# Preset ones for the warming products, and another split of the weights' narrowing, in a fused attention and gated feed-forward kernel

## The chip, the cores and the metric

The kernel runs on one core of one Trainium2 chip. A core has five engines with queues of their own: TensorE (PE) for matrix products, VectorE (DVE), ScalarE (ACT), GpSimd (POOL) and SyncE (SP), the last here used to issue transfers. The metric is the device time of one execution in microseconds. Times below that have a line number are those of the kernel before the change.

## The reference

Attention by a polynomial sketch, then a gated feed-forward layer:

```python
def phi(x):                       # x: batch 4, heads 4, sequence 1088, head dimension 32
    a = einsum('rd,bhsd->bhsr', S1, x)      # r = 8
    b = einsum('rd,bhsd->bhsr', S2, x)
    return outer product of a and b, 64 features
q_p, k_p = phi(q), phi(k)
kv  = einsum('bhsf,bhsd->bhfd', k_p, v)
z   = sum of k_p over s
num = einsum('bhsf,bhfd->bhsd', q_p, kv)
den = einsum('bhsf,bhf->bhs', q_p, z) + 1e-06
x   = (num / den), heads joined: 4352 tokens x 128
out = (sigmoid(x @ w_gate) * (x @ w_val)) @ w_out     # 128 -> 1536 -> 128
```

q, k and v are 32-bit. S1, S2, w_gate, w_val and w_out come as 64-bit floats; the kernel reads them as pairs of 32-bit integers and makes 32-bit floats of them itself.

## The kernel before

**Feed-forward.** The 4352 tokens are cut into chunks of 512 and the 1536 inner columns into 12 blocks of 128. A wave (`w1`, products at L364) makes gate and val of one block for one chunk: two products of 128x512 into one PSUM tile `wave`. ACT takes the sigmoid of gate (`sg`, L372), DVE multiplies with val (`g`, L388). `w2` (L321, tile `moeout`) multiplies the block's g with its w_out and adds over the 12 blocks. `slot` orders them: at each turn the product g of the last wave, then the `moeout` of two waves back, then the next wave. After the twelfth, DVE turns the sum (`o_sb`, L331) and SP writes it out. Products of 32-bit floats appear in the profile as two records each.

**Attention** fills x, transposed (`xT`), batch by batch, between the waves. Batch 0 has nothing to hide behind and goes first: k and q are turned on DVE (`kT` L432, `qT` L443), S is turned on PE (`st`, L812), and from it come `sk` (L823), `kps`, `gram`, `kp`, `dps` (the denominators), `kvz` (k_p times v, L647), `kvd` (a copy on ACT, L683), `ndps` (L717), `nd` (a copy on ACT, L730), `nps` (the numerators, L758) and `xT` (L785). The denominators pass through `dT` (DVE, L750) and `rc` (ACT, L873). The products of ones (`warm`, L262) into a scratch tile give nothing to the result; there are three at the start, one behind `st`, one ahead of `dps`, and one ahead of the first wave.

**Narrowing** (`narrow`) makes 32-bit floats out of pairs in four steps, each placed by hand in the order of the program: step 0 is `cap` on POOL (L97) and `tail` on ACT (L101), the two that read the raw pairs `w_in`; step 1 is two DVE operations on `head` (L105, L109); step 2 is `square` on ACT (L117) and the addition on POOL (L118); step 3 is the DVE write of `w_sb` (L127). Before the change `narrow_01` takes blocks 0 and 1 in three parts (gate and val of 0; gate and val of 1; out of 0 and 1), and `narrow_w(j)` takes gate, val and out of one block j. The engines are scheduled by hand: each executes its instructions in the order in which the program wrote them.

**Loads.** SP issues all loads of weights in one order: gate and val of block 0, v of batch 0, gate and val of block 1, out of 0 and 1, the rest of q, and then gate, val and out by pairs of blocks. The raw pairs of two blocks lie in one tile `w_in` each, and there are six such tiles (`raw`, `bufs=NJ // 2`). Eight semaphores count the landings in turn; the framework puts in the waits for them, by the slices that an instruction reads and that a load writes. The core functions:

Of the kernel before, what the change touches and what calls it, by code (L numbers as in the profile page):

```python
# [9 lines left out]
I32 = mybir.dt.int32  # L10
# [10 lines left out]
def kernel(  # L21
# [30 lines left out]
    const = ctx.enter_context(tc.tile_pool(name="const", bufs=1))  # L52
    ld = ctx.enter_context(tc.tile_pool(name="ld", bufs=1))
    sbA = ctx.enter_context(tc.tile_pool(name="sbA", bufs=2))
    raw = ctx.enter_context(tc.tile_pool(name="raw", bufs=NJ // 2))
    sbN = ctx.enter_context(tc.tile_pool(name="sbN", bufs=1))
    sbG = ctx.enter_context(tc.tile_pool(name="sbG", bufs=6))

# [83 lines left out]
                nc.sync.dma_start(out=rows, in_=s_)  # L142


    w_sb = const.tile([P, 3, NJ, P], F32, tag="w_sb", name="w_sb")
    w_in = {}

    def load_w_in(j0, j1):
        cs = slice(j0 * P, j1 * P)
        n, jj = divmod(j0, 2)  # L150
        if wide and jj == 0:
            w_in[n] = raw.tile([P, 3, 2, P, 2], I32, tag="w_in", name="w_in")
        for i, src in enumerate((moe_w_gate, moe_w_val)):
            if wide:
                nc.sync.dma_start(
                    out=w_in[n][:, i, jj : jj + j1 - j0].rearrange("p j m w -> p (j m w)"),
                    in_=src[:, cs].bitcast(I32),
                )
            else:
                nc.sync.dma_start(  # L160
                    out=w_sb[:, i, j0:j1].rearrange("p j m -> p (j m)"), in_=src[:, cs]
                )

    def load_w_out(n):
        j0, j1 = 2 * n, 2 * n + 2
        cs = slice(j0 * P, j1 * P)
        src = moe_w_out[cs, :].bitcast(I32) if wide else moe_w_out[cs, :]
        nc.sync.dma_start(
            out=w_in[n][:, 2].rearrange("p j m w -> p j (m w)") if wide else w_sb[:, 2, j0:j1],
            in_=src.rearrange("(j p) m -> p j m", p=P),  # L170
        )

    narrowing = {}

    def narrow_w(j, step):
        if not 0 <= j < NJ:
            return
        n, jj = divmod(j, 2)
        if wide:
            if step == 0:  # L180
                narrowing[j] = narrow(
                    w_sb[:, :, j, :], w_in[n][:, :, jj], nc.gpsimd, "acc1" if j < NJ - 2 else None
                )
            next(narrowing[j])


    def narrow_01(part, step):
        if wide:
            if step == 0:
                i = (slice(0, 2), part) if part < 2 else (2, slice(0, 2))  # L190
                narrowing["01", part] = narrow(
                    w_sb[:, i[0], i[1]],
                    w_in[0][:, i[0], i[1]],
                    nc.gpsimd,
                    "acc0" if part else "acc1",
                )
            next(narrowing["01", part])


    def load_rows(src, b, t, parts=((0, T, nc.sync),)):  # L200
# [48 lines left out]
        load_w_in(2 * n, 2 * n + 2)  # L249
        load_w_out(n)  # L250

    ones = const.tile([P, 32], F32, tag="ones")
    nc.vector.memset(ones, 1.0)


    def warm(*cols):
        t = psm.tile([P, 2, 512], F32, tag="wave", name="warm")
        one = [bass.AP(tensor=ones.tensor, offset=ones.offset, ap=[list(ones.ap[0]), [0, n]]) for n in cols]
        x = bass.AP(tensor=ones.tensor, offset=ones.offset, ap=[list(ones.ap[0]), [0, P]])
        for r in one:  # L260
            n = r.shape[-1]
            nc.tensor.matmul(out=t[:, 0, :n], lhsT=x, rhs=r, start=True, stop=True)  # L262

    sig0 = const.tile([P, 1], F32, tag="sig0")
    nc.scalar.activation(out=sig0, in_=ones[:, :1], func=ACTF.Sigmoid)
    warm(512, 512, 128)
    hm = const.tile([P, 2, R], F32, tag="hm")
    nc.vector.memset(hm, 0.0)  # L268
    for h in range(H):
# [44 lines left out]
    def w2(ci, j0, jn, g):  # L314
        t0, tw = tok_chk[ci]
        if j0 == 0:
            moe["sum"] = ci
            moe["acc"] = pso.tile([P, TCH], F32, tag=f"acc{ci % 2}", name="moeout")
        for jj in range(jn):
            j = j0 + jj  # L320
            nc.tensor.matmul(  # L321
                out=moe["acc"][:, :tw],
                lhsT=w_sb[:, 2, j, :],
                rhs=g[:, jj, :tw],
                start=(j == 0),
                stop=(j == NJ - 1),
            )
        if j0 + jn == NJ:
            o_sb = sbA.tile([P, TCH // 32, 32], F32, tag="o_sb", name="o_sb")
            nt = tw // 32  # L330
            nc.vector.transpose(  # L331
                out=o_sb[:, :nt, :].rearrange("p t d -> p (t d)"), in_=moe["acc"][:, :tw]
            )
            c = t0
            while c < t0 + tw:
                b, r = divmod(c, S)
                n = min(t0 + tw - c, S - r) // 32
                u = (c - t0) // 32
                for g4 in range(4):

                    eng = nc.scalar if ci == len(tok_chk) - 1 and g4 % 2 else nc.sync
                    eng.dma_start(
                        out=bass.AP(
                            tensor=out.tensor,
                            offset=out.offset + (b * S + r // 32) * DM + 32 * g4,
                            ap=[[T * DM, 32], [DM, n], [1, 32]],
                        ),
                        in_=o_sb[32 * g4 : 32 * g4 + 32, u : u + n, :],
                    )
                c += n * 32  # L350

    def w1():

        ci = moe["ci"]
        t0, tw = tok_chk[ci]
        jn = TCH // tw
        j0 = moe["w"] * jn
        wv = psm.tile([P, 2, TCH], F32, tag="wave", name="wave")

        tp = tw // 2 if ci == 0 and j0 == 0 else tw  # L360
        for o in range(0, tw, tp):
            for which in range(2):
                for jj in range(jn):
                    nc.tensor.matmul(  # L364
                        out=wv[:, which, jj * tw + o : jj * tw + o + tp],
                        lhsT=w_sb[:, which, j0 + jj, :],
                        rhs=xT[:, t0 + o : t0 + o + tp],
                        start=True,
                        stop=True,
                    )  # L370
        sg = sbG.tile([P, TCH], F32, tag="sg", name="sg", bufs=3)
        nc.scalar.activation(out=sg, in_=wv[:, 0], func=ACTF.Sigmoid)  # L372
        if ci == 0:
            if j0 == 1:
                narrow_01(2, 3)
            if 0 < j0 < NJ - 2:
                narrow_w(j0 + 1, 3)
            narrow_w(j0 + 2, 1)
            narrow_w(j0 + 2, 2)
            if j0 < 3:  # L380
                narrow_w(j0 + 3, 0)
            if j0 > 1:
                narrow_w(j0 + 4, 0)


        def glu():
            g = sbG.tile([P, TCH], F32, tag="g", name="g")
            nc.vector.tensor_tensor(out=g, in0=wv[:, 1], in1=sg, op=MUL)  # L388
            moe["todo"].append((ci, j0, jn, g.rearrange("p (j t) -> p j t", j=jn)))

        moe["gate"] = glu
        moe["w"] += 1
        if j0 + jn == NJ:
            moe["ci"] += 1
            moe["w"] = 0
# [260 lines left out]
    def kv(b, zsum):  # L656
        kvz = KVZ[b] = ps2.tile([P, 2, 512], F32, tag="two", name="kvz")[:, 0]
        for j in [1, 2, 3, 4, 5, 6, 7, 8, 0]:
            kr = 64 if j == 0 else P
            for h in range(H):  # L660
                nc.tensor.matmul(  # L661
                    out=kvz[32 * h : 32 * h + 32, :F],
                    lhsT=v_t[b][:kr, h, j, :],
                    rhs=KP[b][:kr, h // 2, j, h % 2, :],
                    start=(j == 1),
                    stop=(j == 0),
                    skip_group_check=True,
                )
        for h in range(H):
            nc.tensor.matmul(  # L670
                out=kvz[32 * h : 32 * h + 32, F : 2 * F],
                lhsT=ones,
                rhs=zsum[:, h, :],
                start=False,
                stop=True,
                skip_group_check=True,
            )
# [139 lines left out]
        start=True,  # L817
        stop=True,
    )
    warm(128)  # L820
    st_ = st_[:, : 2 * R].rearrange("p (n r) -> p n r", n=2)
    sk = const.tile([P, 2, 2, R], F32, tag="sk")
    nc.vector.tensor_tensor(  # L823
# [28 lines left out]
    mult10 = ab(None, (0, 1, 0), (psm, "wave"))  # L852
    for pi in range(2):
        outer(0, pi, NJK - 1, NJK, eng=nc.gpsimd)
    for part in range(2):
        narrow_01(part, 0)
    spread_z()
    warm(512)
    for pi in range(2):
# [6 lines left out]
    def rest(turn, rc, dT):  # L866
# [5 lines left out]
        nt = rc.shape[1] - 1  # L872
        nc.scalar.activation(out=rc[:, :nt], in_=dT[:, :nt, :2], func=ACTF.Identity, bias=eps)  # L873
        kvd(0)
        narrow_01(0, 1)
        narrow_01(0, 2)
        ndt(0)

    divide = dn(0, 0, rest)
    warm(256)  # L880

    def head1():
        narrow_01(1, 1)
        narrow_01(0, 3)
        narrow_01(1, 2)
        narrow_01(2, 0)
        narrow_w(2, 0)

    divide((0, 4), (4, 8), between=head1)
    narrow_01(1, 3)  # L890
    narrow_01(2, 1)
    narrow_01(2, 2)

    slot(None, 1)
    cq = {}
# [82 lines left out]
```

## Time and profile before

| | |
|---|---|
| median of 12 runs | 305.53 us (305.18 to 309.55) |
| the profiled execution | 305.94 us |
| its span, first to last instruction | 304.2 us |
| mean granted clock of PE | 0.998 |
| transfers | 23.31 MB, mean 77 GB/s over the span |

The span is what the profile divides; some 1.7 us of the execution lie around it. The busiest groups outside PE, as the page has them (line, engine, operation, output and inputs with shapes, count, then busy us, mean ns, and idle us before them with what ended most of it):

```profile
L388 DVE TENSOR_TENSOR g<-wave,sg 128x512 f32<-128x512 f32 x102 | 70.3, 689 | 128.2 <-ACT sg L372 127.9
L118 POOL TENSOR_TENSOR head<-head,tail 128x384 int32<-128x384 int32 (+2 forms) x14 | 13.4, 955 | 17.8 <-DVE head L109 14.7
L262 PE MATMUL warm<-ones 128*128 128x512 f32 (+2 forms) x12 | 6.8, 698 | 1.0 <-DVE hm L268 1.0
L127 DVE SCALAR_TENSOR_TENSOR w_sb<-square,head 128x384 f32<-128x384 f32 (+1 forms) x11 | 5.7, 518 | 3.9 <-POOL head L118 3.9
L101 ACT ACTIVATE tail<-w_in 128x384 int32<-128x384 uint32 (+1 forms) x13 | 6.6, 521 | 0.5 <-DMA w_in<-in_moe_w_gate_dram 0.5
```

Most of the narrowing runs between 9 and 46 us, in the first chunk's waves. Idle time of DVE, ACT and POOL costs nothing by itself; PE is busy 98% of the span.

### The profile page before, as it was taken

The numbers are of one execution on the slowest core, as the hardware profiler recorded it, in microseconds if no ns is written. First come the engines' busy times: TensorE is split into PE (matmuls) and PEld (weight loads), VectorE is DVE, ScalarE is ACT, GpSimd is POOL, SyncE is SP. The second block draws the span as 40 slices with busy tenths as digits, with TensorE's granted clock in tenths as the row PEclk, the third lists the DMA queues.
The fourth block names the chain that finished last, engine by engine and source line by source line (L and its number), as shares of the span: only waits on it lengthen the run. The fifth ranks groups of instructions, "written<-read, shape, count | busy, mean of one in ns | idle before, by whom it ended". The sixth has DMA issues, their size and how long they took to land.

```text
span 304.2 us, 3619 instructions
## 1 busy us (share of the span) xinstructions
PE 297.3 (98%) x1366; PEld 137.0 (45%) x1366; DVE 154.8 (51%) x267; ACT 81.1 (27%) x150; POOL 35.4 (12%) x65
## 2 busy tenths in 40 slices
PE   8899999999999999999999999999999999999995
PEld 3444434443344444434444445434444444444683
DVE  6997798753756444464365443635232223222331
ACT  3556532222222222211222222221222222222220
POOL 1466540600000500000003100000000000000000
PEclk9999999999999999999999999999999999999999
DMA  7992440998402591450004950200010000100021
GB/s 221 356 336 66 126 144 6 163 152 149 147 4 44 127 181 30 79 174 10 0 12 97 187 89 2 36 0 2 0 21 13 0 0 9 28 0 0 7 31 17
DMA packets 29874, 23.31 MB, mean 77 GB/s; under 512 B 20960, under 2 KB 25056, under 8 KB 29856
## 3 DMA queue, kind: packets, MB, share of 16 engines
q1 hardware_dynamic: 25488, 15.21, 18.6%
q0 software_dynamic: 3456, 7.09, 13.7%
q10 hardware_dynamic: 912, 0.77, 0.9%
q8 instruction: 11, 0.18, 0.3%
q14 instruction: 7, 0.06, 0.1%
HBM read 19.80 MB, written 3.26 MB: 76 GB/s over the span
## 4 chain that ended last, share of the span: by engine, by line
PE 74%; DMA 5%; DVE 1%; issue 0%; DVEq 0%
PE wave L364 46%; PE moeout L321 24%; DMA bq<-dq 5%; PE nps L758 1%; PE dps L739 1%; PE kvz L661 1%; DVE qp L639 0%; PE kps L460 0%; PE cqps L606 0%; DVE g L388 0%; PE kvz L670 0%; DVE o_sb L331 0%; PE ndps L717 0%; DVEq L639 0%
## 5 line engine op out<-in xcount | busy, mean ns | idle before, releaser
L364 PE MATMUL wave<-xT,w_sb 128*128 128x512 f32 (+1 forms) x436 | 191.7, 565 | 0.1
L388 DVE TENSOR_TENSOR g<-wave,sg 128x512 f32<-128x512 f32 x102 | 70.3, 689 | 128.2 <-ACT sg L372 127.9
L364 PEld LDWEIGHTS wave<-xT,w_sb 128*128 128x128 f32 x436 | 82.6, 190 | 93.6 <-issue 86.0
L372 ACT ACTIVATE sg<-wave 128x512 f32<-128x512 f32 x102 | 60.9, 597 | 199.5 <-PE wave L364 199.5
L321 PE MATMUL moeout<-g,w_sb 128*128 128x512 f32 (+1 forms) x216 | 105.5, 576 | 0.6 <-DVE w_sb L127 0.3
L321 PEld LDWEIGHTS moeout<-g,w_sb 128*128 128x128 f32 x216 | 39.4, 190 | 44.5 <-issue 37.2
L630 POOL DMA_DIRECT2D qp<-dq x12 | 7.1, 590 | 110.6 <-DMA dq<-cq 68.6
L118 POOL TENSOR_TENSOR head<-head,tail 128x384 int32<-128x384 int32 (+2 forms) x14 | 13.4, 955 | 17.8 <-DVE head L109 14.7
L639 DVE TENSOR_TENSOR qp<-qp,bq 128x1152 f32<-128x1152 f32 (+1 forms) x7 | 9.1, 1295 | 3.9 <-DMA bq<-dq 3.9
L539 DVE TENSOR_TENSOR kp<-kab 128x1152 f32<-128x1152 f32 (+2 forms) x10 | 10.5, 1069 | 0.0
L262 PE MATMUL warm<-ones 128*128 128x512 f32 (+2 forms) x12 | 6.8, 698 | 1.0 <-DVE hm L268 1.0
L109 DVE SCALAR_TENSOR_TENSOR head<-cap,head 128x384 int32<-128x384 int32 (+2 forms) x14 | 7.5, 534 | 0.5
L127 DVE SCALAR_TENSOR_TENSOR w_sb<-square,head 128x384 f32<-128x384 f32 (+1 forms) x11 | 5.7, 518 | 3.9 <-POOL head L118 3.9
L331 DVE STREAM_TRANSPOSE o_sb<-moeout 128x512 f32<-128x512 f32 (+1 forms) x9 | 6.1, 680 | 2.6 <-PE moeout L321 2.5
L630 POOL DMA_DIRECT2D bq<-dq x12 | 6.9, 579 | 0.3
L101 ACT ACTIVATE tail<-w_in 128x384 int32<-128x384 uint32 (+1 forms) x13 | 6.6, 521 | 0.5 <-DMA w_in<-in_moe_w_gate_dram 0.5
L97 POOL TENSOR_SCALAR cap<-w_in 128x384 f32<-128x384 f32 (+1 forms) x13 | 6.5, 509 | 0.0
L785 DVE TENSOR_TENSOR xT<-nps,rb 128x576 f32<-128x576 f32 (+2 forms) x9 | 5.9, 661 | 0.7
L774 DVE STREAM_TRANSPOSE rb<-rc 128x576 f32<-128x576 f32 (+2 forms) x9 | 6.1, 681 | 0.3
L758 PE MATMUL nps<-qp,nd 64*32 64x256 f32 (+1 forms) x128 | 5.5, 401 | 0.4 <-ACT nd L730 0.4
L443 DVE STREAM_TRANSPOSE qT<-kq 128x512 f32<-128x512 f32 (+1 forms) x8 | 5.7, 714 | 0.0
L739 PE MATMUL dps<-qp,zb 128*32 128x256 f32 (+1 forms) x64 | 5.3, 404 | 0.3 <-DVE zb L529 0.2
(74 smaller groups left out, 84.6 us busy)
## 6 DMA issues: line engine op xcount, KB each, us to landing
qp<-dq POOLq DMA_DIRECT2D x12, 288.0 KB, 9.8
bq<-dq POOLq DMA_DIRECT2D x12, 288.0 KB, 9.8
v<-in_v_dram SPq DMA_DIRECT2D x16, 144.0 KB, 6.6
kq<-in_k_dram SPq DMA_DIRECT2D x3, 544.0 KB, 4.2
kq<-in_q_dram SPq DMA_DIRECT2D x3, 544.0 KB, 5.1
w_in<-in_moe_w_out_dram SPq DMA_DIRECT2D x6, 256.0 KB, 7.0
w_in<-in_moe_w_gate_dram SPq DMA_DIRECT2D x5, 256.0 KB, 5.7
w_in<-in_moe_w_val_dram SPq DMA_DIRECT2D x5, 256.0 KB, 4.9
```

What stands on the lines that cost most here:

```text
L109: nc.vector.scalar_tensor_tensor(out=head, in0=cap, scalar=-0x40000000, in1=head, op0=ALU.bitwise_and, op1=ALU.bitwise_or)
L118: nc.gpsimd.tensor_tensor(out=head, in0=head, in1=tail, op=ALU.add)
L262: nc.tensor.matmul(out=t[:, 0, :n], lhsT=x, rhs=r, start=True, stop=True)
L321: nc.tensor.matmul(out=moe["acc"][:, :tw], lhsT=w_sb[:, 2, j, :], rhs=g[:, jj, :tw], start=(j == 0), stop=(j == NJ - 1),)
L364: nc.tensor.matmul(out=wv[:, which, jj * tw + o : jj * tw + o + tp], lhsT=w_sb[:, which, j0 + jj, :], rhs=xT[:, t0 + o : t0 + o + tp], sta ...
L372: nc.scalar.activation(out=sg, in_=wv[:, 0], func=ACTF.Sigmoid)
L388: nc.vector.tensor_tensor(out=g, in0=wv[:, 1], in1=sg, op=MUL)
L539: eng.tensor_tensor(out=KP[b][:, pi, j0:j1].rearrange("p j m (i l) -> p (j m) i l", i=R), in0=bass.AP(tensor=a0.tensor, offset=a0.offset, ...
L630: get.dma_start(out=t[64 * c : 64 * c + 64, n * H * W1 : (n + 1) * H * W1], in_=bass.AP(tensor=d0.tensor, offset=d0.offset, ap=rows + [[1, ...
L639: nc.vector.tensor_tensor(out=q0, in0=q0, in1=half(BQ[b], n), op=MUL)
L739: nc.tensor.matmul(out=dps[32 * h : 32 * h + 32, :w], lhsT=zb[b % 2][:, h, :], rhs=half(QP[b], n)[:, 2 * (h % 2) + h // 2, :], start=True, ...
L758: nc.tensor.matmul(out=t[32 * h : 32 * h + 32, c, :w], lhsT=ND[b][rows, 32 * h : 32 * h + 32], rhs=half(QP[b], n)[rows, 2 * (h % 2) + h // ...
```

## The change

Three things are changed.

The products of ones, the first sigmoid and the sum of z (L670) no longer read a tile `ones` that DVE fills; they read the constant 1.0 that the framework has POOL write before the kernel's first instruction (at L962 in the profile), with a step of zero. The third leading product and the one behind `st` have 256 columns where they had 128.

The raw weights are one tile instead of six, and both it and `w_sb` are laid out as a row of 38 blocks: gate 0 to 11, val 12 to 23, two places unused, out from 26 on.

The narrowing is split otherwise. gate and val of blocks 0, 1 and 2 go by themselves, out of block 0 goes by itself, and from block 3 on one narrowing takes gate j, val j and out of j - 2, which are places j, j + 12 and j + 24, one slice with a step of 12. A last one takes out of 10 and 11.

```diff
-    raw = ctx.enter_context(tc.tile_pool(name="raw", bufs=NJ // 2))
+    raw = ctx.enter_context(tc.tile_pool(name="raw", bufs=1))
...
-    w_sb = const.tile([P, 3, NJ, P], F32, tag="w_sb", name="w_sb")
-    w_in = {}
+    w_sb = const.tile([P, 3 * NJ + 2, P], F32, tag="w_sb", name="w_sb")
+    w_in = raw.tile([P, 3 * NJ + 2, P, 2], I32, tag="w_in", name="w_in") if wide else None
...
-                    out=w_in[n][:, i, jj : jj + j1 - j0].rearrange("p j m w -> p (j m w)"),
+                    out=w_in[:, i * NJ + j0 : i * NJ + j1].rearrange("p j m w -> p (j m w)"),
...
+        to = slice(2 * NJ + 2 + j0, 2 * NJ + 2 + j1)
...
-            out=w_in[n][:, 2].rearrange("p j m w -> p j (m w)") if wide else w_sb[:, 2, j0:j1],
+            out=w_in[:, to].rearrange("p j m w -> p j (m w)") if wide else w_sb[:, to],
...
-    def narrow_01(part, step):
...
+    def narrow_w(part, step):
+        if wide and part in places:
             if step == 0:
...
+                at, bank = places[part]
+                narrowing[part] = narrow(w_sb[:, at], w_in[:, at], nc.gpsimd, bank)
+            next(narrowing[part])
+
+    places = {j: (slice(j, j + 2 * NJ + 1, NJ), "acc1") for j in range(3, NJ - 2)}
+    places.update({j: (slice(j, j + 2 * NJ + 1, NJ), None) for j in range(NJ - 2, NJ)})
+    places.update({("gv", j): (slice(j, j + NJ + 1, NJ), f"acc{1 - j % 2}") for j in range(3)})
+    places["out", 0] = slice(2 * NJ + 2, 2 * NJ + 3), "acc0"
+    places[NJ] = slice(3 * NJ, 3 * NJ + 2), None
...
-    ones = const.tile([P, 32], F32, tag="ones")
-    nc.vector.memset(ones, 1.0)
...
-        x = bass.AP(tensor=ones.tensor, offset=ones.offset, ap=[list(ones.ap[0]), [0, P]])
+        x = nc.const_aps.tensor(1.0, [P, P], F32)
+        for n in cols:
+            r = nc.const_aps.tensor(1.0, [P, n], F32)
...
-    warm(512, 512, 128)
+    warm(512, 512, 256)
...
-                lhsT=w_sb[:, 2, j, :],
+                lhsT=w_sb[:, 2 * NJ + 2 + j, :],
...
         if ci == 0:
-            if j0 == 1:
-                narrow_01(2, 3)
-            if 0 < j0 < NJ - 2:
-                narrow_w(j0 + 1, 3)
-            narrow_w(j0 + 2, 1)
-            narrow_w(j0 + 2, 2)
+            if j0 == 0:
+                narrow_w(("gv", 2), 1)
+                narrow_w(("gv", 2), 2)
+                narrow_w(("out", 0), 3)
+            else:
+                if j0 == 1:
+                    narrow_w(("gv", 2), 3)
+                elif j0 != NJ - 2:
+                    narrow_w(j0 + 1, 3)
+                narrow_w(j0 + 2, 1)
+                narrow_w(j0 + 2, 2)
...
-    warm(128)
+    warm(256)
...
-    for part in range(2):
-        narrow_01(part, 0)
+    narrow_w(("gv", 0), 0)
+    narrow_w(("gv", 1), 0)
...
-        narrow_01(2, 0)
-        narrow_w(2, 0)
+        narrow_w(("out", 0), 0)
+        narrow_w(("gv", 2), 0)
```

In the built program the order of SP's loads is as before, and no load waits for more than it did. The first `tail` on ACT and the first `cap` on POOL (gate and val of block 0) wait for six load semaphores; before, they waited for three.

More of the change, by code (lines that the diff above doesn't have):

```diff
@@ L142, in load_s @@
                 nc.sync.dma_start(out=rows, in_=s_)
-    w_sb = const.tile([P, 3, NJ, P], F32, tag="w_sb", name="w_sb")
-    w_in = {}
+    w_sb = const.tile([P, 3 * NJ + 2, P], F32, tag="w_sb", name="w_sb")
+    w_in = raw.tile([P, 3 * NJ + 2, P, 2], I32, tag="w_in", name="w_in") if wide else None
     def load_w_in(j0, j1):
         cs = slice(j0 * P, j1 * P)
-        n, jj = divmod(j0, 2)
-        if wide and jj == 0:
-            w_in[n] = raw.tile([P, 3, 2, P, 2], I32, tag="w_in", name="w_in")
         for i, src in enumerate((moe_w_gate, moe_w_val)):
@@ L160, in load_w_in @@
                 nc.sync.dma_start(
-                    out=w_sb[:, i, j0:j1].rearrange("p j m -> p (j m)"), in_=src[:, cs]
+                    out=w_sb[:, i * NJ + j0 : i * NJ + j1].rearrange("p j m -> p (j m)"),
+                    in_=src[:, cs],
                 )
@@ L173 @@
     narrowing = {}
[L175 to L179, printed above, removed]
-            if step == 0:
[L181 to L184, printed above, removed]
-    def narrow_01(part, step):
[L188 to L197, printed above, removed]
+    def narrow_w(part, step):
+        if wide and part in places:
+            if step == 0:
+                at, bank = places[part]
[6 more added lines that the diff above has]
+    places[NJ] = slice(3 * NJ, 3 * NJ + 2), None
     def load_rows(src, b, t, parts=((0, T, nc.sync),)):
@@ L250 @@
         load_w_out(n)
-    ones = const.tile([P, 32], F32, tag="ones")
-    nc.vector.memset(ones, 1.0)
     def warm(*cols):
         t = psm.tile([P, 2, 512], F32, tag="wave", name="warm")
-        one = [bass.AP(tensor=ones.tensor, offset=ones.offset, ap=[list(ones.ap[0]), [0, n]]) for n in cols]
-        x = bass.AP(tensor=ones.tensor, offset=ones.offset, ap=[list(ones.ap[0]), [0, P]])
-        for r in one:
-            n = r.shape[-1]
+        x = nc.const_aps.tensor(1.0, [P, P], F32)
+        for n in cols:
+            r = nc.const_aps.tensor(1.0, [P, n], F32)
             nc.tensor.matmul(out=t[:, 0, :n], lhsT=x, rhs=r, start=True, stop=True)
     sig0 = const.tile([P, 1], F32, tag="sig0")
-    nc.scalar.activation(out=sig0, in_=ones[:, :1], func=ACTF.Sigmoid)
-    warm(512, 512, 128)
+    nc.scalar.activation(out=sig0, in_=nc.const_aps.tensor(1.0, [P, 1], F32), func=ACTF.Sigmoid)
+    warm(512, 512, 256)
     hm = const.tile([P, 2, R], F32, tag="hm")
@@ L365, in w1 @@
                         out=wv[:, which, jj * tw + o : jj * tw + o + tp],
-                        lhsT=w_sb[:, which, j0 + jj, :],
+                        lhsT=w_sb[:, which * NJ + j0 + jj, :],
                         rhs=xT[:, t0 + o : t0 + o + tp],
@@ L671, in kv @@
                 out=kvz[32 * h : 32 * h + 32, F : 2 * F],
-                lhsT=ones,
+                lhsT=nc.const_aps.tensor(1.0, [P, 32], F32),
                 rhs=zsum[:, h, :],
@@ L874, in rest @@
         kvd(0)
-        narrow_01(0, 1)
-        narrow_01(0, 2)
+        narrow_w(("gv", 0), 1)
+        narrow_w(("gv", 0), 2)
         ndt(0)
@@ L882, in head1 @@
     def head1():
-        narrow_01(1, 1)
-        narrow_01(0, 3)
-        narrow_01(1, 2)
-        narrow_01(2, 0)
-        narrow_w(2, 0)
+        narrow_w(("gv", 1), 1)
+        narrow_w(("gv", 0), 3)
+        narrow_w(("gv", 1), 2)
+        narrow_w(("out", 0), 0)
+        narrow_w(("gv", 2), 0)
     divide((0, 4), (4, 8), between=head1)
-    narrow_01(1, 3)
-    narrow_01(2, 1)
-    narrow_01(2, 2)
+    narrow_w(("gv", 1), 3)
+    narrow_w(("out", 0), 1)
+    narrow_w(("out", 0), 2)
     slot(None, 1)
```

## The prediction

> **What bounds the kernel now.** I read the page's busy shares first, then the costliest groups, then the order of time around the start, and last the waits of SP's queue, because the change touches only the first 45 us.
>
> ```profile
> span 304.2 us, 3619 instructions
> PE 297.3 (98%) x1366; PEld 137.0 (45%) x1366; DVE 154.8 (51%) x267; ACT 81.1 (27%) x150; POOL 35.4 (12%) x65
> PE   8899999999999999999999999999999999999995
> L364 PE MATMUL wave<-xT,w_sb 128*128 128x512 f32 (+1 forms) x436 | 191.7, 565 | 0.1
> L321 PE MATMUL moeout<-g,w_sb 128*128 128x512 f32 (+1 forms) x216 | 105.5, 576 | 0.6 <-DVE w_sb L127 0.3
> ```
>
> TensorE is the bound: the idle time ahead of its two large groups sums to 0.7 us (0.1 and 0.6) in the whole span. Whatever moves that first product moves the end by as much. It stands here, in the order of time (the columns are start, duration, engine, line, operation):
>
> ```profile
> 9.24 0.81 ACT L101 ACTIVATE tail<-w_in 128x256 int32<-128x256 uint32 x2 [0.46 <-DMA w_in<-in_moe_w_gate_dram]
> ...
> 12.28 0.31 ACT L873 ACTIVATE rc<-dT,eps 128x16 f32<-128x16 f32 x1 [2.23 <-DVE dT L750]
> 12.93 0.27 ACT L683 COPY kvd<-kvz 128x128 f32<-128x128 f32 x1 [0.34 <-PE kvz L647]
> ...
> 13.93 0.67 PE L758 MATMUL nps<-qp,nd 64*32 64x256 f32 x16 [0.35 <-ACT nd L730]
> 14.53 0.70 PE L262 MATMUL warm<-ones 128*128 128x256 f32 x2
> ```
>
> The first wave product starts at 15.18. Ahead of it on ACT stands the narrowing of blocks 0 and 1 (tail, 9.24), and behind that, in the same queue, the reciprocal's input rc, the copy kvd and the copy nd. Note what ended the 0.46 us before the tail: a gate load. The first tail reads gate and val of block 0 alone, issued at 1.93 and 2.41; but the gate load of block 1 was issued at 4.97, and in the built program this tail waits for it too. Its slice (gate 0 and val 0, two blocks apart) has gate 1 lying between them, and the wait covers what lies between.
>
> The other rows I need are SP's. It issues the last loads of gate at 16.01, and is then held (waits of SP's queue, 20 to 28 us: waiter, what it waited for, us in total, times, longest):
>
> ```profile
> 16.01 0.33 SPq L155 DMA_DIRECT2D w_in<-in_moe_w_gate_dram  x1
> ...
> 20.23 0.31 SPq L215 DMA_DIRECT2D v<-in_v_dram  x1
> SPq L630 <- DMA dq<-cq: 5.0, 1, 5.0
> SPq L630 <- DMA w_in<-in_moe_w_gate_dram: 1.6, 1, 1.6
> ```
>
> So the gate load of blocks 10 and 11 landed at 20.54 + 1.6 = 22.2 us. (Then 5.0 more to 27.2, where the next issue stands at 27.27: the sum closes.)
>
> [...] rc, kvd, nd stand in program order. [...] weight loads for the 512-column ones follow each other by 0.86 us (1.97, 2.83, 3.68), while in the steady part they follow by 0.43 (26.16, 26.59, 27.02). [...]
>
> **The change part by part.**
>
> 1. *w_in becomes one tile of 38 blocks: gate 0-11, val 12-23, two unused, then out.* This is the part that decides. The first narrowing now takes blocks 0 and 12. Between them lie all twelve gate blocks. The changed program's ACT and POOL queues show it: the first tail and the first cap wait for six load semaphores where three stood before, each counted up to the last gate load that uses it, the latest being gate 10-11. Those loads are issued by SP in the old order with no new wait, and SP depends on nothing that ACT now holds (its next wait on compute is the end of kvz on PE, at 12.9, which ACT does not feed). So they land when they did: 22.2. The first tail moves from 9.24 to 22.2. Behind it wait, on ACT: the second tail, rc, kvd, squares, nd; on POOL: both caps; DVE waits at the head of block 0 after dT (11.75), PE at ndps. Two tails take 0.81: rc at 23.0. From rc (12.28) to the first wave (15.18) took 2.90 before; the weights' own path, cap 0.4, DVE 0.25 + 0.42, POOL 0.73, DVE 0.42, is 2.2 plus handovers and runs beside it. First wave at 25.9: **+10.7**. Nothing gives it back, since PE is full afterwards. If the landing moves by 0.7 either way, so does this.
>
> 2. *PE's clock.* PE has nothing between kvz's end (12.87) and ndps (23.6), 10.7 us. I take the half rate from there. ndps 0.33 and nps 0.67 contain some 0.5 of streaming: +0.5. After that the waves run at half rate until about 4.2 us after nps began (the length of the first slow ones, 0.96 to 5.17), that is from 26.4 to 28.6-29: 2.4 us of time does 1.2 us of work: +1.2. The slow PE hides the 0.3 that moeout waited for w_sb: -0.3. **+1.4**; bounds 0.5 (nps counts early and clock is back at 27) and 2.6 (half rate for 4.2 us after 26.4, and nothing hidden).
>
> 3. *out is narrowed two blocks later, with gate and val of j go out of j-2.* moeout of j-2 stands one product (0.86 us) ahead of wave j on PE, so it needs the same w_sb write 0.86 earlier. Before, w_sb for blocks 5 to 9 ended at 28.32, 30.95, 33.57, 36.19, 38.82, and moeout of 3 to 7 started at 27.88, 30.45, 33.02, 35.60, 38.17: each would now be late by 0.4 to 0.65. These are not added: the loop DVE w_sb, 105, 109, POOL head, w_sb turns in 2.62 us by itself against PE's 2.57, so lateness is carried, up to 0.65. Block 11 is worse: w_sb ended at 46.02, moeout of 9 started at 44.94 before; late by 1.08, of which 0.65 has been paid, and the 0.27 that wave 11 waited anyway goes: 0.2 more. Block 12 (out 10 and 11) adds on DVE 0.28 + 0.42 + 0.42, on POOL 0.5 + 0.73, and ends near moeout of 10: 0.1. Together near 0.9; the slow PE at the start lets the loop gain a little on it: **+0.7**; bounds 0 (loop far ahead) and 1.7 (each block pays anew).
>
> 4. *Ones from the constant.* One memset (0.09) and PE's wait for it go: first product 0.1 earlier. The third leading product has 256 columns for 128: at half rate +0.4, so st, at 5.20, comes up to 0.3 later; the one behind st adds up to 0.2 ahead of kps. All this ends by 13.5 and is covered by the wait to 22.2: **0**; without cover up to 0.5.
>
> 5. *Narrower first pieces.* out of block 0 alone (128 columns for 256) and gate and val of 2 (256 for 384) save about 0.5 on DVE and 0.6 on POOL between 16 and 20 of the old time. PE gained at most the 0.3 already taken in step 2: **0**.
>
> Sum: 10.7 + 1.4 + 0.7 = 12.8. The profiled execution took 305.94, of which 1.7 lies around its span of 304.2; it would give 318.7. The median, 305.53, is 0.4 lower: 305.5 + 12.8 = **318.3**.
>
> **The rivals.**
> *The wait bites alone* (chance 0.13): PE gets its clock back at once and w_sb stays ahead: 10.7 or a bit less, 316.0. For: ones and nps precede the first wave; against: 10.7 us of idle.
> *Everything dear* (0.11): clock slow for longer, or loads landing near 23, and each late w_sb paid: 10.7 + 2.6 + 1.7 = 15, 320.5 to 321. For: the loop of 2.62 has no slack[...].
> *The other side* (0.05): the long slice's wait ends before it matters, as it would if the last gate load landed by about 9.8 us, ahead of rc; then the head is unmoved, moeout's 0.3 goes, part 3 returns as much, and the time is 305.2: no change. Against: that load is not even issued until 16.01.
> My forecast, all three terms near their middles, has 0.71.
>
> **How the numbers follow.** The likeliest gives 318.3. The range takes the first rival's middle and half of the dear case: 315.9 to 320.6. What a measurement here can tell from no change is about 0.5%, 1.5 us. Slower holds all but the other side: 0.95; of the rest, same 0.03, faster 0.02.
>
> **What would show it.** In the changed kernel's profile: the first tail near 22.2, waiting some 13 us on a gate load; first wave near 26; PE's third slice of 40 (16 to 24 us) empty; weight loads for the first wave products longer than 0.19; moeout waiting for w_sb in sum 0.5 to 1; everything after 60 us shifted by a constant. Wrong if the tail starts near 9 (then no part of this holds), or if the shift keeps changing after 60 us.

## The result, and the profile after

The changed kernel takes 318.09 us (median of 11 runs, 316.66 to 319.43) against 305.49 (median of 47). The ratio is 1.0405, with a 95% interval of 1.0384 to 1.0426: slower, by 12.6 us. 318.3 was predicted, with 315.9 to 320.6 as the range.

The page of the changed kernel: its span, the busy shares, PE's busy tenths and granted clock in 40 slices of 7.9 us, and the group of the copy `kvd`'s reader.

```profile
span 316.3 us, 3624 instructions
PE 299.5 (95%) x1366; PEld 137.9 (44%) x1366; DVE 155.9 (49%) x269; ACT 80.8 (26%) x152; POOL 35.8 (11%) x67
...
PE   8509999899999999999999999999999999999995
PEclk9956999999999999999999999999999999999999
...
L709 PE MATMUL ndps<-ident,kvd 128*128 128x128 f32 x7 | 1.6, 302 | 10.4 <-ACT kvd L675 10.4
```

PE's busy time has hardly grown (297.3 to 299.5); the span has grown by 12.1. The third slice, 16 to 24 us, is empty, and nearly all new idle time stands before one product, `ndps`, which waits for an ACT copy. The clock row shows a second thing: the granted clock of slices 3 and 4 (15.8 to 31.6 us) is 5 and 6 tenths.

The order of time around the start (start, duration, engine, line, operation, and in brackets the idle time before it and what ended that):

```profile
11.63 0.44 DVE L742 STREAM_TRANSPOSE dT<-dps 128x256 f32<-128x256 f32 x1
...
22.01 0.75 ACT L101 ACTIVATE tail<-w_in 128x256 int32<-128x256 uint32 x2 [13.35 <-DMA w_in<-in_moe_w_out_dram]
22.11 0.78 POOL L97 TENSOR_SCALAR cap<-w_in 128x256 f32<-128x256 f32 x2 [12.17 <-DMA v<-in_v_dram]
...
22.66 0.29 ACT L865 ACTIVATE rc<-dT,eps 128x16 f32<-128x16 f32 x1
22.86 0.25 ACT L675 COPY kvd<-kvz 128x128 f32<-128x128 f32 x1
...
23.16 0.48 PE L709 MATMUL ndps<-ident,kvd 128*128 128x128 f32 x1 [10.41 <-ACT kvd L675]
...
23.99 1.11 PE L750 MATMUL nps<-qp,nd 64*32 64x256 f32 x16 [0.35 <-ACT nd L722]
```

The first tail, at 9.24 before, stands at 22.01, and 13.35 us of idle time on ACT stand ahead of it. dT is ready at 12.1, kvz at 12.8, and their readers rc and kvd, behind the tail in ACT's queue, follow only after 22.6. The name in the bracket, a load of out, is one of several loads whose landings were counted near that moment; that the tail waited for a gate load has to be read from SP's queue (waits from 18 to 40 us):

```profile
SPq L622 <- DMA w_in<-in_moe_w_gate_dram: 1.4, 1, 1.4
```

SP's next issue after the last v load waits for the last gate load, as before the change, and that load landed at 21.9, just ahead of the tail.

### The profile page after: what moved, and what is told of

Read it like the earlier page. It is cut to its first block, busy times and chain, and to the rows that moved or that the text cites. A ratio compares the mean times of both kernels' runs of the same rounds, so it can differ in the third digit from the quotient of the medians.

```text
span 316.3 us, 3624 instructions
## 1 busy us (share of the span) xinstructions
PE 299.5 (95%) x1366; PEld 137.9 (44%) x1366; DVE 155.9 (49%) x269; ACT 80.8 (26%) x152; POOL 35.8 (11%) x67
## 4 chain that ended last, share of the span: by engine, by line
PE 88%; DMA 6%; DVE 2%; POOL 1%; ACT 1%; issue 1%; SPq 1%; ACTq 0%
PE wave L351 54%; PE moeout L308 28%; DMA w_in<-in_moe_w_out_dram 3%; DMA w_in<-in_moe_w_gate_dram 2%; PE nps L750 2%; PE kvz L653 1%; PE dps L731 1%; DMA kq<-in_k_dram 1%; POOL head L118 1%; PE cqps L598 1%; PE kps L452 1%; DVE w_sb L127 0%; SPq L206 0%; PE warm L249 0%; PE ndps L709 0%
## 5 line engine op out<-in xcount | busy, mean ns | idle before, releaser
L351 PEld LDWEIGHTS wave<-xT,w_sb 128*128 128x128 f32 x436 | 83.9, 193 | 93.3 <-issue 89.2
L118 POOL TENSOR_TENSOR head<-head,tail 128x384 int32<-128x384 int32 (+3 forms) x15 | 13.7, 915 | 20.9 <-DVE head L109 9.7
L709 PE MATMUL ndps<-ident,kvd 128*128 128x128 f32 x7 | 1.6, 302 | 10.4 <-ACT kvd L675 10.4
L105 DVE TENSOR_SCALAR head<-cap 128x384 int32<-128x384 int32 (+3 forms) x15 | 5.4, 360 | 10.5 <-POOL cap L97 10.5
L531 DVE TENSOR_TENSOR kp<-kab 128x1152 f32<-128x1152 f32 (+2 forms) x10 | 10.5, 1068 | 0.0
L101 ACT ACTIVATE tail<-w_in 128x384 int32<-128x384 uint32 (+2 forms) x14 | 6.7, 500 | 13.4 <-DMA w_in<-in_moe_w_out_dram 13.4
L249 PE MATMUL warm<-const-float32-1.0 128*128 128x512 f32 (+1 forms) x12 | 7.5, 754 | 0.8 <-PEq L954 0.8
L97 POOL TENSOR_SCALAR cap<-w_in 128x384 f32<-128x384 f32 (+2 forms) x14 | 6.6, 479 | 12.2 <-DMA v<-in_v_dram 12.2
L109 DVE SCALAR_TENSOR_TENSOR head<-cap,head 128x384 int32<-128x384 int32 (+3 forms) x15 | 7.4, 496 | 0.5
L127 DVE SCALAR_TENSOR_TENSOR w_sb<-square,head 128x384 f32<-128x384 f32 (+2 forms) x11 | 5.4, 494 | 2.6 <-POOL head L118 2.6
```

Of the source, the lines that this page charges most:

```text
L101: nc.scalar.activation(out=tail, in_=lo, func=ACTF.Copy, scale=2.0**-29)
L109: nc.vector.scalar_tensor_tensor(out=head, in0=cap, scalar=-0x40000000, in1=head, op0=ALU.bitwise_and, op1=ALU.bitwise_or)
L118: nc.gpsimd.tensor_tensor(out=head, in0=head, in1=tail, op=ALU.add)
L351: nc.tensor.matmul(out=wv[:, which, jj * tw + o : jj * tw + o + tp], lhsT=w_sb[:, which * NJ + j0 + jj, :], rhs=xT[:, t0 + o : t0 + o + tp ...
L531: eng.tensor_tensor(out=KP[b][:, pi, j0:j1].rearrange("p j m (i l) -> p (j m) i l", i=R), in0=bass.AP(tensor=a0.tensor, offset=a0.offset, ...
```

## The experiments

Two questions stood open: whether the wait of the long slice, and not the new split of the narrowing, makes the 12.6 us; and how much the slow clock and the later `out` add.

**pair_tiles.** The new split stays, but the raw weights lie in six tiles of two blocks again; row 2 of each holds the out blocks of the pair before.

```diff
-    w_in = raw.tile([P, 3 * NJ + 2, P, 2], I32, tag="w_in", name="w_in") if wide else None
+    w_in = [
+        raw.tile([P, 3, 2, P, 2], I32, tag="w_in", name="w_in") for _ in range(NJ // 2)
+    ]
...
+    def raw_of(part):
+        if part == NJ:
+            return w_in[0][:, 2]
+        if part == ("out", 0):
+            return w_in[1][:, 2, :1]
+        if isinstance(part, tuple):
+            return w_in[part[1] // 2][:, :2, part[1] % 2]
+        return w_in[part // 2][:, :, part % 2]
...
-                narrowing[part] = narrow(w_sb[:, at], w_in[:, at], nc.gpsimd, bank)
+                narrowing[part] = narrow(w_sb[:, at], raw_of(part), nc.gpsimd, bank)
```

> The changed kernel with the raw weights in six tiles of two blocks again, the out rows of each holding the pair before, so that every slice of a narrowing stays inside one pair. All else as changed. Theory A (the long slice's wait for the last gate load is the cost): first tail near 9.3, first wave near 15.2, time 305.3 to 306.5, what is above before being the later out. Rival B (splitting the narrowing and taking out two blocks later is the cost): 310 or more, with moeout waiting for w_sb several us.

Measured: 305.95 us (22 runs), ratio to before 1.0021, interval 1.0003 to 1.0038. The order of time on ACT, and the start of the first wave on PE:

```profile
9.20 0.81 ACT L101 ACTIVATE tail<-w_in 128x256 int32<-128x256 uint32 x2 [0.65 <-DMA w_in<-in_moe_w_gate_dram]
...
14.95 3.71 PE L364 MATMUL wave<-xT,w_sb 128*128 128x256 f32 x12
```

With short slices the tail is back at 9.20 and 12 of the 12.6 us are gone, with every other part of the change still in. `w_sb` keeps its one tile and its long slices here, and no such wait follows from them; it is the tile that the loads write that matters. Theory A holds, rival B falls.

**before_one_tile.** The counterpart: the kernel before, with its own split and ones, and only the tile of the raw weights changed.

```diff
-    w_in = {}
+    w_in = raw.tile([P, 3, NJ, P, 2], I32, tag="w_in", name="w_in")
...
-                    w_sb[:, :, j, :], w_in[n][:, :, jj], nc.gpsimd, "acc1" if j < NJ - 2 else None
+                    w_sb[:, :, j, :], w_in[:, :, j], nc.gpsimd, "acc1" if j < NJ - 2 else None
...
-                    w_in[0][:, i[0], i[1]],
+                    w_in[:, i[0], i[1]],
```

> The kernel before, with one change: the raw weights in one tile, so that the first narrowing's slice spans all gate blocks. The split and the ones are those of before. Theory A: first tail near 22, first wave near 26, PE's clock lost in between, time 316.5 to 317.5 (10.9 for the first wave, 0.7 for the slow clock after it). Rival B: 305 to 306.

Measured: 317.0 us (4 runs), ratio 1.0373, interval 1.0325 to 1.042. Waits of PE in sum, and ACT's first tail:

```profile
PE ndps L714 <- ACT kvd L680: 10.2, 1, 10.2
...
21.93 0.75 ACT L101 ACTIVATE tail<-w_in 128x256 int32<-128x256 uint32 x2 [13.17 <-DMA w_in<-in_moe_w_out_dram]
```

The layout of the raw tile, in a kernel otherwise untouched, brings the whole wait. Together with pair_tiles it shows the tile to be both enough and needed. The built programs say the same: the first tail waits for three load semaphores in pair_tiles, as in the kernel before, and for six in before_one_tile, as in the changed kernel. The first wave, at 25.97, came 10.8 later than before. The slow clock (0.50 from 16.29 to 29.94) was dearer than expected, 1.3 up to the third wave (6.33 against 5.01) and not 0.7, but 0.4 of it came back by the thirteenth.

**gates_first.** If the tail waits for the last gate load, an earlier last gate load must shorten the wait by as much. The changed kernel, with SP's order altered:

```diff
-    for n in range(1, NJ // 2):
-        load_w_in(2 * n, 2 * n + 2)
-        load_w_out(n)
+    for i in range(2):
+        for n in range(1, NJ // 2):
+            load_w_in(2 * n, 2 * n + 2, i)
+    for n in range(1, NJ // 2):
+        load_w_out(n)
```

> The changed kernel with SP's loads in another order: from block 2 on all of gate, then all of val, then all of out. The last gate load is then the fifth of these and not the thirteenth, and lands near 16. Theory A: first tail near 16, first wave near 20, time 310 to 312. Rival D (the first narrowing waits for the whole tile, or ACT is held by something else): 317 to 319.

Measured: 311.72 us (4 runs), ratio 1.0194, interval 1.0155 to 1.0234.

```profile
15.79 0.75 ACT L101 ACTIVATE tail<-w_in 128x256 int32<-128x256 uint32 x2 [7.26 <-DMA w_in<-in_moe_w_val_dram]
...
19.67 4.10 PE L355 MATMUL wave<-xT,w_sb 128*128 128x256 f32 x12
```

The tail came 6.22 us sooner (22.01 to 15.79), the first wave 6.37 (26.04 to 19.67). From the tail's start to 23.0 the DMA engines stayed 90% busy or more and moved 2.3 MB, an estimate from the profile's GB/s in slices of 0.4 us; the four loads of v that follow the weights hold 0.6 MB, so most of the 2.6 MB of val and out from block 2 on came after the tail had started. It isn't the tile as a whole that is waited for, though the bracket names a val load. Rival D falls. By medians the time fell by 6.4. That this is so near the tail's gain is in part chance: the profiled execution, at 310.47 the fastest of the four, is 7.6 below the changed kernel's. Its stretch at a granted clock of 0.50 was shorter too (3.42 us against 13.66), and from the first wave to the third it took another 0.9 less (4.79 against 5.69); the three other executions had a lower mean granted clock (0.988 to 0.989 against 0.992).

**after_busy_pe.** The changed kernel, with ones on PE during its wait, to price the clock.

```diff
         kvd(0)
+        for _ in range(12):
+            warm(512)
         narrow_w(("gv", 0), 1)
```

> The changed kernel with twelve more products of ones (512 columns) on PE behind kvz, which fill its wait. Theory A with the clock as a term of its own: the clock stays whole from 13 to 26, nps back from 1.11 to 0.67 us, first wave near 25.4, second and third waves at full rate: 1.0 to 1.6 us less than the changed kernel, 316.5 to 317.1. Rival C (the slow clock is hidden by DVE's writes of w_sb anyway): 317.8 to 318.3.

Measured: 316.93 us (4 runs), 1.16 below the changed kernel by medians, ratio to before 1.0387, interval 1.0335 to 1.044. The time alone is thin, since the changed kernel's own interval in ratios, 1.0384 to 1.0426, overlaps; the trace is plain:

```profile
12.74 10.61 PE L249 MATMUL warm<-const-float32-1.0 128*128 128x512 f32 x24
...
21.80 0.76 ACT L101 ACTIVATE tail<-w_in 128x256 int32<-128x256 uint32 x2 [13.08 <-DMA v<-in_v_dram]
...
22.45 0.30 ACT L865 ACTIVATE rc<-dT,eps 128x16 f32<-128x16 f32 x1
...
23.19 0.27 PE L709 MATMUL ndps<-ident,kvd 128*128 128x128 f32 x1
...
23.82 0.67 PE L750 MATMUL nps<-qp,nd 64*32 64x256 f32 x16 [0.35 <-ACT nd L722]
...
25.50 3.71 PE L351 MATMUL wave<-xT,w_sb 128*128 128x256 f32 x12 [0.38 <-DVE xT L777]
```

The granted clock was 1.00 from 12.9 to 33, where the changed kernel had 0.50 from 15.18 to 28.84. ndps went from 0.48 to 0.27, nps from 1.11 back to 0.67, the first wave from 26.04 to 25.50, and the third wave from 31.73 to 29.90. Of the 0.54 at the first wave, 0.21 is no matter of the clock: the tail itself started sooner in this execution (21.80 against 22.01). From rc to the first wave it is 3.05 us here and 3.38 in the changed kernel (22.66 to 26.04). So the clock's price is 0.33 ahead of the first wave and 1.29 from the first to the third (4.40 against 5.69), 1.6 in all by then. Rival C falls in the trace. The eleven executions of the changed kernel point the same way: the three with the highest mean granted clock (0.981 to 0.984) took 316.66 to 317.41 us, the eight others (0.976 to 0.978) 317.54 to 319.43. (The profiled execution of after_busy_pe, 320.3 us, ran into another wait at 87 us, told of in the last section; the three other runs lie between 316.05 and 317.06.)

**before_const_ones.** The part that the prediction set at nothing, alone: the kernel before with the ones from the constant and the wider warming products.

```diff
-    ones = const.tile([P, 32], F32, tag="ones")
-    nc.vector.memset(ones, 1.0)
...
-    warm(512, 512, 128)
+    warm(512, 512, 256)
...
-    warm(128)
+    warm(256)
```

> The kernel before with the ones alone changed: products of ones and the first sigmoid read the constant 1.0, leading ones of 512, 512 and 256 columns, 256 behind st. Theory A: first product 0.2 us earlier, st and kps within 0.1 of before, first wave within 0.3 of 15.2, time 305.0 to 305.7. Rival E (the wider ones hold up st and what follows): first wave 0.3 to 0.5 later and 305.8 to 306.3.

Measured: 305.74 us (22 runs) against 305.58 on the same chip, ratio 0.9978, interval 0.9957 to 0.9999: no difference that matters (by medians it is 0.16 above, by the ratio 0.2% below). First product at 0.78 for 0.96, first wave at 15.06 for 15.18. The median lies between the ranges of the two theories; the first wave, sooner and not later, is against rival E.

**pair_out_one_back.** What is left of pair_tiles over before, 0.66 us, was put to `out` being needed one product too early. Here a narrowing from block 2 on takes out of j - 1, and the loads of out are grouped to fit.

```diff
-    places = {j: (slice(j, j + 2 * NJ + 1, NJ), "acc1") for j in range(3, NJ - 2)}
+    places = {j: (slice(j, j + 2 * NJ + 1, NJ), "acc1") for j in range(2, NJ - 2)}
...
-                lhsT=w_sb[:, 2 * NJ + 2 + j, :],
+                lhsT=w_sb[:, 2 * NJ + 1 + j, :],
```

> As pair_tiles, but a narrowing from block 2 on takes gate j, val j and out of j - 1 (loaded in that grouping), and the last takes out of 11 alone; out of block 0 still goes by itself. moeout of j - 1 stands behind wave j on PE, so out is no longer needed ahead of gate and val. Theory F (the 0.66 us by which pair_tiles is above before is moeout waiting for w_sb one product too early): moeout's waits for w_sb gone, the step from one wave to the next 2.57 to 2.58 us instead of 2.63, time 304.9 to 305.4. Rival G (the rest is the extra narrowing, with its two more operations on DVE and POOL): 305.7 to 306.1, as pair_tiles.

Measured: 305.65 us (14 runs) against 305.58, ratio 0.999, interval 0.9962 to 1.0018. The order of time on PE shows three waves and the `moeout` between them, pair_tiles first:

```profile
33.49 1.88 PE L364 MATMUL wave<-xT,w_sb 128*128 128x512 f32 x4
35.21 1.08 PE L321 MATMUL moeout<-g,w_sb 128*128 128x512 f32 x2
36.12 1.88 PE L364 MATMUL wave<-xT,w_sb 128*128 128x512 f32 x4
```

```profile
33.31 1.88 PE L366 MATMUL wave<-xT,w_sb 128*128 128x512 f32 x4
35.03 1.02 PE L323 MATMUL moeout<-g,w_sb 128*128 128x512 f32 x2
35.88 1.88 PE L366 MATMUL wave<-xT,w_sb 128*128 128x512 f32 x4
```

The step is 2.63 with out of j - 2 and 2.57 with j - 1, and the wait of 0.56 that moeout had for w_sb in pair_tiles (at 45.23) is gone; a wave waits 0.25 for it instead (at 45.64). From the third wave to the thirteenth pair_tiles takes 29.52 us and this one 28.82. So the trace is with theory F. The times don't settle it: 305.65 lies above the range of F and just below that of G, and the intervals of the two kernels (1.0003 to 1.0038 and 0.9962 to 1.0018) overlap. It is the best form of the change that was run, and it is level with the kernel before, not ahead of it.

## Why the prediction was right

By starts of waves in the traces, in us. A wave is two products; the thirteenth is the first of chunk 1.

| stretch | before | after | after_busy_pe | before_one_tile | gates_first | pair_tiles |
|---|---|---|---|---|---|---|
| to the first wave | 15.18 | 26.04 | 25.50 | 25.97 | 19.67 | 14.95 |
| first to third | 5.01 | 5.69 | 4.40 | 6.33 | 4.79 | 4.41 |
| third to thirteenth | 28.56 | 29.70 | 29.85 | 28.16 | 29.20 | 29.52 |
| thirteenth to the last | 248.70 | 248.18 | 252.08 | 248.18 | 248.34 | 248.18 |

1. *The wait*, set at 10.7. after_busy_pe, which has it without the slow clock, has its first wave at 25.50, that is 10.3 later than before; with the tail 0.21 later, as in the changed kernel, it is 10.5. The mechanism was as told, and the three kernels with other tiles or loads confirm its links: last gate load, tail, rc and kvd in ACT's queue, first wave. The small excess came from the landing, 21.9 and not 22.2; the way from rc to the first wave was a little longer than forecast, 3.05 and not 2.90.

2. *The clock*, set at 1.4 net: 1.7 in itself, less 0.3 of hidden waiting. In itself it cost 1.6, and part 5 below takes more off it than was credited. That the gap would bring the half rate, and for how long, was the author's estimate: the trace of before has no such gap (behind its first product PE waits for 0.4 us at most). The trace of the changed kernel has a granted clock of 0.50 from 15.18 to 28.84; the prediction had it back at 28.6 to 29. That this fitted is luck. It counted 4.2 us from the start of nps, but the half rate ended 4.85 us after nps began here, 3.03 in gates_first (17.62 to 20.65) and 6.02 in before_one_tile (23.92 to 29.94): no one time from nps fits the three.

3. *The later out*, set at 0.7. Third to thirteenth wave: 29.70 against 28.56, 1.1 us. The size was low, and its place was wrong. The prediction let the narrowing loop carry lateness of up to 0.65 through blocks 5 to 9 and gave block 11 0.2 more. In the trace the loop lost 0.24 (third to tenth wave 19.08 against 18.84). Where the clock was whole (1.00 in the mean of pair_tiles, 1.00 up to 33 us in after_busy_pe) it lost 0.55 (pair_tiles, 19.39) and 0.56 (after_busy_pe, 19.40), so the forecast was right that the slow start of PE lets the loop gain a little. But from the tenth wave to the thirteenth another 0.90 was lost (10.62 against 9.72; 0.4 to 0.7 in gates_first, pair_tiles and after_busy_pe), where some 0.3 was forecast for blocks 11 and 12:

```profile
57.44 1.13 PE L308 MATMUL moeout<-g,w_sb 128*128 128x512 f32 x2 [0.71 <-DVE w_sb L127]
...
60.47 1.12 PE L308 MATMUL moeout<-g,w_sb 128*128 128x512 f32 x2 [0.19 <-DVE w_sb L127]
```

These are moeout of blocks 9 and 10 of the changed kernel. The wait of 0.71 is for the narrowing of block 11, whose write stands on DVE behind the attention's dT, rc and rb; the 0.19 is for the added narrowing of out 10 and 11.

4. *The ones*, set at nothing: before_const_ones agrees.

5. *Narrower first pieces*, set at nothing beyond the 0.3 credited under the clock. First to third wave takes 4.40 in after_busy_pe and 4.41 in pair_tiles, against 5.01 before: 0.6 gained, twice what was credited. pair_out_one_back, which narrows block 2 at 384 columns as before, takes 4.40 too (15.11 to 19.51), so the gain comes from out of block 0 going by itself (the ones alone leave it at 5.02, in before_const_ones). In the changed kernel the slow clock spends it: 5.69. It is also why pair_tiles, in spite of 0.96 lost on out, starts its thirteenth wave no more than 0.13 after before (48.88 against 48.75). The 0.66 between their medians is more than these traces account for, and its interval, from a ratio of 1.0003 on, nearly reaches no difference.

Sum at the thirteenth wave: 10.53 + 1.62 - 0.61 + 1.14 = 12.68, which is 61.43 - 48.75. It must close, since the terms are differences of the same starts; how it is shared out rests on after_busy_pe. The spans differ by 12.1 alone, because the profiled execution of before, 305.94, was itself 0.45 above its median: between two waves near 76 us it lost 0.5 (first rows below), where before_const_ones (second rows) did not. After 60 us the shift changes by this once.

```profile
73.98 1.88 PE L364 MATMUL wave<-xT,w_sb 128*128 128x512 f32 x4
76.11 1.12 PE L321 MATMUL moeout<-g,w_sb 128*128 128x512 f32 x2 [0.26 <-DVE g L388]
77.08 1.88 PE L364 MATMUL wave<-xT,w_sb 128*128 128x512 f32 x4
```

```profile
73.83 1.88 PE L361 MATMUL wave<-xT,w_sb 128*128 128x512 f32 x4
...
76.41 1.88 PE L361 MATMUL wave<-xT,w_sb 128*128 128x512 f32 x4
```

So the 12.8 came near the measured 12.6 for a reason that was right, since the wait is over four fifths of it, and with some luck in the rest, where errors offset each other: the wait 0.2 too dear, the clock with the pieces 0.4 too dear (1.4 against 1.0), the out 0.4 too cheap. The rival that had the wait alone (316.0) left out a clock that is shown to cost; the dear case had the half rate last to 30.6, and it ended at 28.84; the other side would have needed the last gate load near 9.8, and it landed at 21.9.

## What to carry to other kernels

In these programs a strided slice of a large tile that loads write was waited for as if it were all that lies between its ends. Merging tiles so that one slice can reach across them can make the first user wait for the last load: compare the semaphores that each reader waits for, with their counts, before and after a change of layout. What the wait cost here is what stood behind it in the program: ACT took up rc and kvd behind the tail, at 22.66 and 22.86, though what they read was ready at 12.1 and 12.8, and the attention needed both. The gap on PE was paid again in its clock: 10.4 us of gap, then a granted clock of 0.50 up to 28.84, which cost 1.6 us. With the gap filled (after_busy_pe) the clock was 1.00 from 12.9 to 33.

## What the runs showed of the hardware that was not expected

Four stretches at half rate were read from the traces, each with a granted clock of 0.50. They differ in length and in where they begin; the gap is the wait of PE next to the start of the stretch.

| run | gap on PE (us) | half rate | length | PE busy in it |
|---|---|---|---|---|
| after | 10.41, to 23.16 | 15.18 to 28.84 | 13.66 | 5.33 |
| before_one_tile | 10.23, to 23.09 | 16.29 to 29.94 | 13.65 | 6.50 |
| gates_first | 4.33, to 16.93 | 17.23 to 20.65 | 3.42 | 3.06 |
| after_busy_pe | 1.93, to 88.80 | 88.99 to 92.41 | 3.42 | 3.42 |

In the first two the clock fell during the gap, in the other two 0.30 and 0.19 us after PE had work again. What sets the start and the length of a stretch these traces don't settle. At the very start the traces give no slow clock (before, 1.00 to 5.20 us: 1.00), though the weight loads 0.86 us apart there (prediction) follow each other half as fast as in the steady part, 0.43.

The last row came with the shortest gap. In the profiled execution of after_busy_pe, DVE waited 5.3 us for a transfer of bq, an operand of the attention's product qp, and PE then waited 1.93 for DVE; at 88.99 the clock went to 0.50 for 3.42 us.

```profile
84.98 1.88 PE L351 MATMUL wave<-xT,w_sb 128*128 128x512 f32 x4
88.80 1.91 PE L308 MATMUL moeout<-g,w_sb 128*128 128x512 f32 x2 [1.93 <-DVE g L380]
90.50 2.83 PE L351 MATMUL wave<-xT,w_sb 128*128 128x512 f32 x4
```

A late transfer of bq was met in that execution (longest wait of DVE 5.3 us) and, milder, in the profiled one of before (3.6); whether it makes the spread between executions of one kernel (305.04 to 310.85) was not tried.
